# A fused block-sorted attention and PReLU feed-forward kernel: batch 0 without key padding, zeros moved from q to K, and a new instruction order

## The chip, the cores and the metric

The kernel runs on one core of a Trainium2 chip. The metric is device time in microseconds of one execution; lower is better. The engines are PE (matmul), PEld (its weight loads), DVE (vector), ACT (activations), POOL (general) and SP (which only issues DMAs here). "L853" is line 853 of the kernel's source.

## The reference

Attention has 4 batches, 8 heads, 768 positions and 64 dimensions per head. Each head's 8 x 8 matrix is normalised five times (Sinkhorn) and mixes the 8 blocks of 96 keys and values; query block i then attends to mixed block i alone.

```python
for _ in range(5):
    P = P - np.max(P, axis=-1, keepdims=True)
    P = np.exp(P)
    P = P / (np.sum(P, axis=-1, keepdims=True) + 1e-09)
    P = P / (np.sum(P, axis=-2, keepdims=True) + 1e-09)
...
k_sorted = np.einsum('bhij,bhjcd->bhicd', P, k_b).reshape(B, H, S, D)
v_sorted = np.einsum('bhij,bhjcd->bhicd', P, v_b).reshape(B, H, S, D)
...
scores = scale * np.matmul(q_b, k_sb.transpose(0, 1, 2, 4, 3))
scores = scores - np.max(scores, axis=-1, keepdims=True)
attn = np.exp(scores)
attn = attn / (np.sum(attn, axis=-1, keepdims=True) + 1e-09)
return np.matmul(attn, v_sb).reshape(B, H, S, D).astype(np.float32)
...
h = x @ w_in                       # x: 3072 x 512, w_in: 512 x 2048
g = np.maximum(h, 0.0) + alpha * np.minimum(h, 0.0)
return (g @ w_out).astype(np.float32)
```

## The kernel before

**An order written out.** The body does not emit instructions at once. It adds operations to a graph, each with what it reads and writes, and numbers them in the order in which they were added. Three tables then decide everything: `ORDER` lists for each of the five engines the numbers of its operations in the order in which they run, `BANKS` gives each accumulator tile its PSUM bank, and entries such as `11.1` in PE's list are fillers (`filler`, L1009: eleven products of the identity with 512 columns, into bank 1), which only keep PE running. An operation waits for the semaphores of what it depends on, and what stands behind it on its engine waits with it. An operation marked `EITHER` may stand in ACT's list or in DVE's.

**Groups.** There are 32 groups `g` of 96 positions, 8 to a batch. Batch 0 (`near`) and batches 1 to 3 (`far`) take different ways, to start early in the one and to save PE in the other.

**Opening, batch 0.** A first run of `BURST` products of 32 x 32 zeros (L907) and fillers keep PE running. SP loads `sort_net` (`P32`, L402) and `moe_alpha` (`alphaR`, L404). POOL's queue loads q, v and k of batch 0, then k of batch 1, the four row blocks of `w_in`, then v and `w_out`. `consts` (L478 on) builds the identity (DVE memset, POOL select, ACT copy to `identb`) and masks from it by DVE reductions. `sinkhorn` (L552 on) runs five rounds on DVE with one exp on ACT in each, and leaves `Pb`. `spread0` (L584) spreads it with three selectors held in `w_out_bf` until the weights arrive; DVE makes the block matrices `BDQ` (L589) and `BDV` (L594). `prep_q` (L645) transposes q on PE, `prep_k0` (L661) mixes and transposes k in 6 units, and `prep_v` (L716) mixes v in 8 units of 8 products each, with a strided slice of `hT` as weights and 64 moving columns; ACT or DVE copies each result out of PSUM (through the helper at L397). Batch 0 has its 96 keys of a block laid out as 4 x 32, of which 24 are filled; the rest are zeros or copies (L495, L497, L670).

**One group of attention** (`attention`). For batch 0, L755 makes scores with q in rows, DVE takes their maximum (L762, `nm`), L770 makes the scores again transposed, L781 subtracts the maxima by a product with the identity, ACT takes the exp (L801, `ET`), and L812 multiplies by v, with a 65th column for the sum. DVE divides (L817, L820, `xq`) and PE turns the result (L834) into `xT`. For batches 1 to 3, L752 makes scores with full rows: q is staged in `QN` with zeros beside each head (L508), turned by DMA into `QTz` (L440), and multiplied by K of two heads at once, in 8 products of 96 columns. ACT takes the exp (L789), a DMA turns it (L794), and L812 follows. K and v of these batches are prepared by POOL copies into zero-padded stages (`conv_k` L677, `conv_v`), one product per unit (`prep_k` L689, `prep_v` L716) and a copy out of PSUM.

**The feed-forward part** runs in chunks of 192 or 384 positions: `ffn1` (L853 on PE, relu on ACT at L860 into one of three `t1`, then L863 on DVE into `hT`) and `ffn2` (L885, a copy out, and the store at L896). Its steps are set between those of the attention.

Of the kernel before, what the change touches and what calls it, by code (L numbers as in the profile page):

```python
# [13 lines left out]
NB = 8  # L14
# [9 lines left out]
BK = (128, 112)  # L24
LK = 4 * NB * 128
NE = 3
VSL = 4
EPS = 1e-9
BURST = 140
# [13 lines left out]
        723 759 662 894 659 893 890 660 661 889 663 819 787 788 818 918 917""",  # L43
    "sync": """
# [3 lines left out]
        1127 1098 1118 1090 1058 1148 1172 1214 1226 1193 1220 1232""",  # L48
    "pe": """
# [17 lines left out]
        1224 1217 1218 1229 1230""",  # L67
    "act": """
# [10 lines left out]
        1180 1183 1195 1198 1147 1204 1207 1225 1219""",  # L79
    "dve": """  # L80
# [13 lines left out]
        1163 1151 1178 1160 1187 1192 1166 1175 1171 1184 1202 1181 1196 1199 1208 1205 1213 1231""",  # L94
}
BANKS = (
    "0720176402566007103123674545623016702014516040740232332571154023556674710151666723230371765023127466"
    "7345562601566762045563520172323073704233472267005451247552145562703761201777760440167073416745102212"
    "4567503020451227731314512700026654567764370120171140356567274267567010450223343406134451717670102147"
    "562372753011225033452370700112467116304617335716342532617524"  # L100
# [221 lines left out]
def bass_sinkhorn_attn__then__act_prelu_kernel(  # L322
# [40 lines left out]
    one0 = sb("one0", [128, 1], F32)  # L363
# [6 lines left out]
    QN = sb("QN", [128, 6, 8, 128], BF16)  # L370
# [3 lines left out]
    QTz = [sb("QTz%d" % n, [128, 2, 4, S], BF16) for n in range(2)]  # L374
# [38 lines left out]
    d_qn = [dma_sem("qn%d" % h) for h in range(H)]  # L413
# [10 lines left out]
    def load_q(b, prio):  # L424
        if b == 0:
            o, i = quarters(hT, 8192, HR, q)
            G.add(POOL, lambda e: e.dma_start(o, i), load_us, w=[("QS", 0)], prio=prio, dma=(d_q, 0), kind="load")
            return
        for h in range(H):
            G.add(POOL, lambda e, h=h: e.dma_start(  # L430
                AP(QN, h * 128 + (h // 4) * 64, [[6144, 128], [1024, 6], [1, 64]]),
                AP(q.tensor, b * HB + h * S * D, [[D, 128], [128 * D, 6], [1, D]])),
                660, r=[("QN0", h)] + paced(13, h // 2) * (b == 3), w=[("QN", h)], prio=prio,
                dma=(d_qn[h], 0), kind="load")
# [45 lines left out]
    def consts():  # L480
# [26 lines left out]
        for h in range(H):  # L507
            G.add(POOL, lambda e, h=h: e.memset(  # L508
                AP(QN, h * 128 + (1 - h // 4) * 64, [[6144, 128], [1024, 6], [1, 64]]), 0.0),
                430, w=[("QN0", h)], prio=-21)  # L510
# [538 lines left out]
```

## Time and profile before

| | |
|---|---|
| median of 3 runs | 239.11 us (237.74, 239.11, 239.56) |
| the profiled execution's own time | 237.91 us |
| its span, first to last instruction | 236.2 us |
| PE busy | 228.7 us (97%) |
| DVE, ACT, POOL busy | 167.2, 151.8, 104.3 us |
| mean granted PE clock | 0.986 |
| DMA | 31.35 MB, mean 133 GB/s |

The profile is of one execution; 1.7 us of its time lie outside its span. Rows of the timeline and of the chain begin with the start and the length in us, then the engine (in the timeline) or the engine and what is written (in the chain); "x8" is the number of instructions that were merged. A busy PE is not PE at its peak, since ends of products are modelled. In the windows, the clock is the share of the full PE clock that was granted.

### The profile page before, as it was taken

The page shows a single profiled execution, that of the slowest core. Times are in us where ns is not written, and L with a number is a line of the kernel's source. Part 1 is how long each engine was busy: PE and PEld are TensorE (multiplying, and loading weights), DVE is VectorE, ACT ScalarE, POOL GpSimd, SP SyncE. Part 2 cuts the span into 40 slices and gives each one's busy share as a digit, 9 for nine tenths or more (in the row PEclk, how much of TensorE's full clock was granted, in tenths as well). Part 3 has the DMA queues.
Part 4 walks back from the last instruction along what each step waited for, and adds up shares of the span by engine and source line. Part 5 has one row for each costly group of instructions (what it writes and reads, how often), then busy time and mean ns, then how long its engine had stood idle before and what let it go on. Part 6 is the DMA issues. An engine that isn't in the chain of part 4 may idle for free.

```text
span 236.2 us, 5977 instructions
## 1 busy us (share of the span) xinstructions
PE 228.7 (97%) x2379; PEld 144.9 (61%) x2379; DVE 167.2 (71%) x344; ACT 151.8 (64%) x421; POOL 104.3 (44%) x153
## 2 busy tenths in 40 slices
PE   5999989999999999999999999999999999999995
PEld 3469868866566666566665666565655556455553
DVE  5774499997699788896797687684877558634741
ACT  4356648988598796687867758457758564433331
POOL 7939929997399997431778880000000000000000
PEclk9998599999999999999999999999999999999999
DMA  5999999996999999999828999842282691400024
GB/s 82 213 218 208 208 190 209 220 153 46 179 181 132 106 127 181 220 231 180 160 80 84 102 132 143 164 81 51 60 118 75 154 166 44 140 4 0 0 92 179
DMA packets 72381, 31.35 MB, mean 133 GB/s; under 512 B 64528, under 2 KB 67360, under 8 KB 72352
## 3 DMA queue, kind: packets, MB, share of 16 engines
q0 software_dynamic: 23808, 13.63, 42.6%
q1 hardware_dynamic: 48544, 17.33, 36.8%
q8 instruction: 19, 0.31, 0.6%
q14 instruction: 10, 0.08, 0.1%
HBM read 27.28 MB, written 6.29 MB: 142 GB/s over the span
## 4 chain that ended last, share of the span: by engine, by line
PE 82%; DMA 7%; DVE 5%; ACT 3%; issue 1%; SPq 0%; POOLq 0%
PE ps L853 32%; PE ps L885 31%; PE ps L716 4%; PE ps L752 4%; PE ps L812 3%; DMA ET<-Esb 3%; DMA hT<-in_q_dram 3%; PE ps L781 2%; DVE hT L863 2%; PE ps L689 1%; ACT ET L801 1%; DVE outstg L397 1%; PE ps L834 1%; PE ps L755 1%; DMA out_dram<-outstg 1%
## 5 line engine op out<-in xcount | busy, mean ns | idle before, releaser
L863 DVE SCALAR_TENSOR_TENSOR hT<-t,omaT,ps 128x384 bf16<-128x384 f32 (+1 forms) x144 | 76.7, 562 | 30.8 <-ACT t L860 29.1
L853 PE MATMUL ps<-xT,w_in_bf 128*128 128x384 bf16 (+1 forms) x576 | 95.6, 308 | 0.2 <-DVE rec L817 0.2
L885 PE MATMUL ps<-w_out_bf,hT 128*128 128x512 bf16 (+1 forms) x400 | 93.4, 371 | 0.1
L860 ACT ACTIVATE t<-ps 128x384 f32<-128x384 f32 (+1 forms) x144 | 61.5, 458 | 43.8 <-PE ps L853 33.7
L853 PEld LDWEIGHTS ps<-xT,w_in_bf 128*128 128x128 bf16 x576 | 51.8, 98 | 29.6 <-ACT xT L397 0.4
L885 PEld LDWEIGHTS ps<-w_out_bf,hT 128*128 128x128 bf16 x400 | 36.5, 98 | 32.9 <-DVE VS L397 0.2
L789 ACT ACTIVATE Esb<-ps,nf 96x96 bf16<-96x96 f32 x192 | 46.1, 345 | 6.4 <-DVE nf L762 6.2
L397 POOL COPY VDz<-VST 64x384 bf16<-64x384 bf16 x40 | 34.1, 852 | 9.8 <-DMA VST<-in_v_dram 6.0
L677 POOL COPY KSz<-KS 64x512 bf16<-64x512 bf16 x36 | 22.0, 612 | 8.9 <-DMA KS<-in_k_dram 3.6
L762 DVE TENSOR_REDUCE nf<-ps 96x8 f32<-96x768 f32 x24 | 22.7, 948 | 3.5 <-PE ps L752 3.4
L430 POOL DMA_DIRECT2D QN<-in_q_dram x24 | 20.0, 838 | 6.5 <-DMA QTz<-QN 6.5
L820 DVE TENSOR_TENSOR xq<-ps,rec 96x512 bf16<-96x512 f32 x32 | 21.7, 681 | 0.4
L812 PEld LDWEIGHTS ps<-VS,ET 112*128 112x128 bf16 (+1 forms) x256 | 11.4, 99 | 5.2 <-ACT ET L801 0.9
L812 PE MATMUL ps<-VS,ET 112*128 112x65 bf16 (+1 forms) x256 | 13.4, 196 | 1.1 <-ACT ET L801 0.6
L397 DVE COPY outstg<-ps 128x512 f32<-128x512 f32 (+1 forms) x14 | 9.3, 667 | 7.1 <-PE ps L885 4.8
L752 PEld LDWEIGHTS ps<-KT,QTz 128*96 128x96 bf16 x192 | 11.9, 125 | 3.6 <-ACT VS L397 0.5
L397 ACT ACTIVATE VS<-ps 112x512 bf16<-112x512 f32 (+1 forms) x18 | 12.0, 697 | 3.1 <-PE ps L716 2.9
L397 ACT ACTIVATE KT<-ps 128x512 bf16<-128x512 f32 x17 | 9.8, 600 | 4.1 <-PE ps L661 2.4
L752 PE MATMUL ps<-KT,QTz 128*96 128x96 bf16 x192 | 12.4, 208 | 0.0
L817 DVE RECIPROCAL rec<-ps 96x8 f32<-96x8 f32 x32 | 6.3, 200 | 8.3 <-PE ps L812 8.1
L762 DVE TENSOR_REDUCE nm<-ps 96x8 bf16<-96x768 f32 x8 | 7.6, 949 | 5.9 <-PE ps L755 5.8
L397 ACT ACTIVATE outstg<-ps 128x512 f32<-128x512 f32 (+1 forms) x11 | 6.4, 579 | 7.9 <-PE ps L885 7.9
(101 smaller groups left out, 183.6 us busy)
## 6 DMA issues: line engine op xcount, KB each, us to landing
out_dram<-outstg SPq DMA_DIRECT2D x23, 256.0 KB, 2.6
KS<-in_k_dram POOLq DMA_DIRECT2D x3, 768.0 KB, 9.8
QN<-in_q_dram POOLq DMA_DIRECT2D x24, 96.0 KB, 3.7
w_in_bf<-in_moe_w_in_dram POOLq DMA_DIRECT2D x4, 512.0 KB, 9.2
w_out_bf<-in_moe_w_out_dram POOLq DMA_DIRECT2D x2, 1024.0 KB, 16.3
VST<-in_v_dram POOLq DMA_DIRECT2D x4, 384.0 KB, 13.5
hT<-in_q_dram POOLq DMA_DIRECT2D x1, 768.0 KB, 7.3
hT<-in_v_dram POOLq DMA_DIRECT2D x2, 384.0 KB, 6.2
```

The source lines that it names most:

```text
L397: return e.activation(o, i, ACTF.Copy) if e is nc.scalar else e.tensor_copy(o, i)
L430: G.add(POOL, lambda e, h=h: e.dma_start(AP(QN, h * 128 + (h // 4) * 64, [[6144, 128], [1024, 6], [1, 64]]), AP(q.tensor, b * HB + h * S * ...
L677: G.add(POOL, lambda e, hp=hp: e.tensor_copy(AP(KSz, hp * 64 * 3072 + u % 3 * 1024 + hp * 64, [[3072, 64], [128, 8], [1, 64]]), AP(KS[n], ...
L752: inst = e.matmul(o, AP(QTz[n], hp * 3072 + h4 * 768 + i * 96, [[6144, 128], [1, 96]]), AP(KT[n], (h4 * 8 + i) * bk, [[LK, 128], [64, 2], ...
L762: G.add(DVE, lambda e: e.tensor_reduce(AP(nx, 0, [[8, 96], [4, 2], [1, 4]]), AP(ps, X.at(), [[LP, 96], [X.step, 2], [96, 4], [1, 96]]), Ax ...
L789: inst = e.activation(AP(Esb[me], p * 128, [[1024, 96], [64, 2], [1, 48]]), AP(ps, X.at((p % 4) * 96) + p // 4 * X.step, [[LP, 96], [48, 2 ...
L812: inst = e.matmul(AP(ps, Z.at(h4 * 68) + hp * Z.step, [[LP, 128], [1, 65]]), AP(ET[et], pos(h4, hp) * 96, [[800, nk], [1, 128]]), AP(VS[n] ...
L820: G.add(DVE, lambda e: e.tensor_tensor(out=AP(xq[me], 0, [[512, 96], [256, 2], [64, 4], [1, 64]]), in0=AP(ps, Z.at(), [[LP, 96], [Z.step, ...
L853: inst = e.matmul(AP(ps, T.at(), [[LP, 128], [1, n]]), AP(w_in_bf, kt * DFF + ft * 128, [[KT_TILES * DFF, 128], [1, 128]]), AP(xT, kt * XR ...
L860: G.add(ACT, lambda e: e.activation(AP(t1[tb], 0, [[384, 128], [1, n]]), AP(ps, T.at(), [[LP, 128], [1, n]]), ACTF.Relu, scale=-1.0), t_ac ...
L863: G.add(DVE, lambda e: e.scalar_tensor_tensor(out=AP(hT, ft * RING + tok % RING, [[FT_TILES * RING, 128], [1, n]]), in0=AP(t1[tb], 0, [[38 ...
L885: inst = e.matmul(AP(ps, T.at(), [[LP, 128], [1, n]]), AP(hT, ft * RING + tok % RING, [[FT_TILES * RING, 128], [1, 128]]), AP(w_out_bf, ft ...
```

## The change

Seven things change together, and the three tables are written anew (the numbers of operations shift with the body):

- Batch 0 is dense: 96 keys per block with no padding. K of batch 0 is written at stride 24, the POOL copy at L670, the memsets at L497 and the masked column of ones (`one0`, an ACT step) go, and the second scores, the subtraction and the exp take 96 keys where they took 128.
- `prep_v` of batch 0 reads 128 strided columns as weights over 96 keys (the last 32 come from q's part of `hT` and are not used), and seven of the eight products of a unit have 128 moving columns, of which the second 64 are written over by the next product.
- In batches 1 to 3 K and not q is zero-padded: `QN` and the turned q have half their size, `QN` has two buffers, K of two heads stands in 192 columns with zeros (`zero_k`, two POOL memsets per buffer), and the first scores are 4 products of 192 columns where they were 8 of 96. Each copy of a K unit out of PSUM becomes two, of 64 partitions each.
- `spread0` has one PSUM tile and one operation for each of its three selectors.
- `NE` is 4 where it was 3 (buffers of exp, its turned form and `xq`), and `BURST` is 165 where it was 140.
- In the new order SP issues `alphaR` ahead of `sort_net`; DVE has the maximum of `sort_net` ahead of the memset of the identity; 16 of the 48 transposes of q stand ahead of the spread and 32 behind it; the last selector is copied on ACT behind the first copy of q; one of the six units of k stands behind four units of v.
- Fillers are 9, 13 and 2 where they were 11, 11, 3, 1 and 3. POOL has all six `BDM` and `BDV` products of batches 1 to 3, of which DVE had three. Of the K copies of batches 1 to 3 ACT has 25 and DVE 11 (14 and 4 before).

```diff
-BK = (128, 112)
-LK = 4 * NB * 128
-NE = 3
+BK = (96, 192)
+LK = 4 * NB * 192
+NE = 4
-BURST = 140
+BURST = 165
...
-                AP(QN, h * 128 + (h // 4) * 64, [[6144, 128], [1024, 6], [1, 64]]),
+                AP(QN[b % 2], h % 4 * 128 + h // 4 * 64, [[3072, 128], [512, 6], [1, 64]]),
...
-            AP(QTz[n], t * 128, [[6144, 128], [768, 8], [1, 128]]),
-            AP(QN, t * 1024, [[6144, 128], [1, 1024]])),
+            AP(QT[n], t * 128, [[3072, 128], [768, 4], [1, 128]]),
+            AP(QN[n], t * 512, [[3072, 128], [1, 512]])),
...
     def spread0(prio):
-        T = G.bank(1, "P")
-        def f(e):
-            inst = None
-            for x in range(3):
+        T = [G.bank(1, "P") for _ in range(3)]
+        for x in range(3):
+            def f(e, x=x):
+                inst = None
...
-        if u == 1:
-            G.add(POOL, lambda e: e.tensor_copy(AP(KT[0], 24, [[LK, 128], [32, 128], [1, 8]]),
-                                                AP(KT[0], 0, [[LK, 128], [32, 128], [1, 8]])), 1150,
-                  r=[("KT", 0, 0), ("KT", 0, 1)], w=["KTpad"], prio=prio + 0.1)
+    def zero_k(n, prio):
+        z = KT[n].bitcast(F32)
+        for hp in range(2):
+            G.add(POOL, lambda e, hp=hp: e.memset(
+                AP(z, hp * 64 * (LK // 2) + (1 - hp) * 48, [[LK // 2, 64], [96, 32], [1, 48]]), 0.0),
+                1600, w=[("KTz", n, hp)], prio=prio)
...
-        o = AP(KT[n], 8 * u, [[LK, 128], [BK[1], 32], [64, 2], [1, 8]])
-        G.add(EITHER, lambda e: copy(e, o, AP(ps, T.at(), [[LP, 128], [2, 32], [1, 2], [64, 8]])),
-              t_either(512), r=[T], w=[("KT", n, u)], prio=prio)
+        for hp in range(2):
+            G.add(EITHER, lambda e, hp=hp: copy(
+                e, AP(KT[n], hp * (64 * LK + 96) + 8 * u, [[LK, 64], [192, 32], [48, 2], [1, 8]]),
+                AP(ps, hp * 64 * LP + T.at(), [[LP, 64], [2, 32], [1, 2], [64, 8]])),
+                t_either(512), r=[T], w=[("KT", n, u, hp)], prio=prio)
...
+                w = 2 if dd < 7 else 1
+                inst = e.matmul(AP(ps, T.at(dd * 64), [[LP, 128], [1, 64 * w]]),
+                                AP(hT, 8 * u + dd, [[HR, 128], [64, 128]]),
+                                AP(BDV, 0, [[256, 128], [0, w], [1, 64]]))
...
+                if far:
+                    inst = e.matmul(sc(2 * h4, 96, 192), AP(QT[n], h4 * 768 + i * 96, [[3072, 128], [1, 96]]),
+                                    AP(KT[n], (h4 * 8 + i) * bk, [[LK, 128], [1, bk]]))
+                    continue
```

More of the change, by code (lines that the diff above doesn't have):

```diff
@@ L369, in bass_sinkhorn_attn__then__act_prelu_kernel @@
     hT = sb("hT", [128, FT_TILES, RING], BF16)
-    QN = sb("QN", [128, 6, 8, 128], BF16)
+    QN = [sb("QN%d" % n, [128, 6, 4, 128], BF16) for n in range(2)]
     KS = [sb("KS%d" % n, [128, 3072], BF16) for n in range(2)]
@@ L373, in bass_sinkhorn_attn__then__act_prelu_kernel @@
     VDz = sb("VDz", [128, VSL * 8 * 128], BF16)
-    QTz = [sb("QTz%d" % n, [128, 2, 4, S], BF16) for n in range(2)]
+    QT = [sb("QT%d" % n, [128, 4, S], BF16) for n in range(2)]
     KT = [sb("KT%d" % n, [128, LK], BF16) for n in range(2)]
@@ L411, in bass_sinkhorn_attn__then__act_prelu_kernel @@
     load_us = 3720
-    d_qn = [dma_sem("qn%d" % h) for h in range(H)]
+    d_qn = [dma_sem("qn%d" % h) for h in range(2 * H)]
     d_qt = [dma_sem("qt%d" % t) for t in range(6)]
@@ L494, in consts @@
         for th in range(2):
-            G.add(POOL, lambda e, th=th: e.memset(AP(zh, th * 64 * HR // 2 + (1 - th) * 2048, [[HR // 2, 64], [1, 2048]]), 0.0),
-                  1990, w=[("VDo", th)], prio=-95.2)
-            G.add(POOL, lambda e, th=th: e.memset(AP(zh, th * 64 * HR // 2 + th * 2048 + 768, [[HR // 2, 64], [1024, 2], [1, 256]]),
-                                                  0.0), 560, w=[("VDp", th)], prio=-95.2)
+            G.add(POOL, lambda e, th=th: e.memset(AP(zh, th * 64 * HR // 2 + (1 - th) * 1536, [[HR // 2, 64], [1, 1536]]), 0.0),
+                  1450, w=[("VDo", th)], prio=-95.2)
         zv, zk = VDz.bitcast(F32), KSz.bitcast(F32)
@@ L506, in consts @@
             G.add(DVE, lambda e, n=n: e.memset(AP(ET[n], 768, [[800, 128], [1, 32]]), 0.0), 100, w=[("ETp", n)], prio=-88)
[L507 to L510, printed above, removed]
-        G.add(DVE, lambda e: e.memset(AP(VS[1], 64, [[64 * 65, 128], [65, 64]]), 0.125), 110, w=[("VS1", 1)], prio=-30)
+        zero_k(1, -21)
+        for n in range(2):
+            G.add(DVE, lambda e, n=n: e.memset(AP(VS[n], 64, [[64 * 65, 128], [65, 64]]), 0.125), 110, w=[("VS1", n)],
+                  prio=(-69, -30)[n])
         def red(o, src, w, prio=-70, ax=AxisListType.X):
@@ L532, in consts @@
               prio=-67)
-        red(one0[:, :], AP(identf, 0, [[128, 128], [32, 4], [1, 24]]), "one0", -69, AxisListType.XY)
-        G.add(ACT, lambda e: e.activation(AP(VS[0], 64, [[64 * 65, 128], [65, 64]]), AP(one0, 0, [[1, 128], [0, 64]]),
-                                          ACTF.Copy, scale=0.125),
-              490, r=["one0"], w=[("VS1", 0)], prio=-60)
         G.add(ACT, lambda e: copy(e, AP(selk, 0, [[512, 32], [16, 32], [1, 16]]),
@@ L577, in spread0 @@
     def spread0(prio):
-        T = G.bank(1, "P")
-        def f(e):
-            inst = None
-            for x in range(3):
+        T = [G.bank(1, "P") for _ in range(3)]
+        for x in range(3):
+            def f(e, x=x):
+                inst = None
                 for j in range(8):
-                    inst = e.matmul(AP(ps, T.at(x * 8), [[LP, 128], [1, 8]]), AP(w_out_bf, x * 1024 + j * 128, [[WR, 32], [1, 128]]),
+                    inst = e.matmul(AP(ps, T[x].at(), [[LP, 128], [1, 8]]),
+                                    AP(w_out_bf, x * 1024 + j * 128, [[WR, 32], [1, 128]]),
                                     AP(Pb, j, [[64, 32], [8, 8]]), start=(j == 0), stop=(j == 7))
-            return inst
-        G.add(PE, f, 24 * 26, r=["Pb"] + [("sel0", x) for x in range(3)], w=[T], prio=prio, mode=1)
+                return inst
+            G.add(PE, f, 8 * 26, r=["Pb", ("sel0", x)], w=[T[x]], prio=prio, mode=1)
         for x in range(2):
@@ L649, in prep_q @@
         G.add(PE, f, 8 * 58, r=[("QS", 0), "identb"], w=[T], prio=prio, mode=4)
-        G.add(EITHER, lambda e: copy(e, AP(QTz[0], 8 * u, [[6144, 128], [24, 128], [1, 8]]),
+        G.add(EITHER, lambda e: copy(e, AP(QT[0], 8 * u, [[3072, 128], [24, 128], [1, 8]]),
                                      AP(psb, 2 * T.at(), [[2 * LP, 128], [1, 128], [128, 8]])),
@@ L665, in prep_k0 @@
         G.add(PE, f, 4 * 58, r=[("KS", 0), ("KS", 0, 0), ("BDQ", 0), ("BDQ", 1)], w=[T], prio=prio, mode=4)
-        G.add(EITHER, lambda e: copy(e, AP(KT[0], 4 * u, [[LK, 128], [32, 128], [1, 4]]),
+        G.add(EITHER, lambda e: copy(e, AP(KT[0], 4 * u, [[LK, 128], [24, 128], [1, 4]]),
                                      AP(ps, T.at(), [[LP, 128], [1, 128], [128, 4]])),
-              t_either(512), r=[T], w=[("KT", 0, u)], prio=prio)
-        if u == 1:
-            G.add(POOL, lambda e: e.tensor_copy(AP(KT[0], 24, [[LK, 128], [32, 128], [1, 8]]),
-                                                AP(KT[0], 0, [[LK, 128], [32, 128], [1, 8]])), 1150,
-                  r=[("KT", 0, 0), ("KT", 0, 1)], w=["KTpad"], prio=prio + 0.1)
+              t_either(512), r=[T], w=[("KT", 0, u, hp) for hp in range(2)], prio=prio)
+    def zero_k(n, prio):
[4 more added lines that the diff above has]
+                1600, w=[("KTz", n, hp)], prio=prio)
     def conv_k(b, u, prio):
@@ L713, in f @@
             for dd in range(8):
-                z = AP(VDz, (u % VSL * 8 + dd) * 128, [[VSL * 1024, 128], [1, 128]]) if b else \
-                    AP(hT, 8 * u + dd, [[HR, 128], [64, 128]])
-                inst = e.matmul(AP(ps, T.at(dd * 64), [[LP, 128], [1, 64]]), z,
-                                AP(BDV, b * 64, [[256, 128], [1, 64]]))
-            return inst
-        G.add(PE, f, 235 if b else 8 * 60,
-              r=[(x, th) for x in ("VD", "VDo", "VDp") for th in range(2)] * (b == 0) +
-              [("VDz", u % VSL, th) for th in range(2)] * (b > 0) + [("BDV", b)], w=[T], prio=prio)
+                if b:
+                    inst = e.matmul(AP(ps, T.at(dd * 64), [[LP, 128], [1, 64]]),
+                                    AP(VDz, (u % VSL * 8 + dd) * 128, [[VSL * 1024, 128], [1, 128]]),
+                                    AP(BDV, b * 64, [[256, 128], [1, 64]]))
+                    continue
[3 more added lines that the diff above has]
+                                AP(BDV, 0, [[256, 128], [0, w], [1, 64]]))
+            return inst
+        G.add(PE, f, 235 if b else 8 * 89,
+              r=[(x, th) for x in ("VD", "VDo") for th in range(2)] * (b == 0) + [("QS", 0)] * (b == 0) +
+              [("VDz", u % VSL, th) for th in range(2)] * (b > 0) + [("BDV", b)], w=[T], prio=prio, mode=0 if b else 7)
         G.add(EITHER, lambda e: copy(e, AP(VS[n], 8 * u, [[64 * 65, nk], [65, 64], [1, 8]]),
@@ L734, in attention @@
         bk = BK[far]
-        nk = 112 if far else 128
+        nk = 112 if far else 96
         pos = (lambda h4, hp: 2 * h4 + hp) if far else (lambda h4, hp: 4 * hp + h4)
-        kt_keys = [("KT", n, u) for u in range(6)]
-        qt_keys = [("QTzt", n, t) for t in range(i * 96 // 128, (i * 96 + 95) // 128 + 1)] if far else \
+        kt_keys = [("KT", n, u, hp) for u in range(6) for hp in range(2)] + [("KTz", n, hp) for hp in range(2)]
+        qt_keys = [("QTt", n, t) for t in range(i * 96 // 128, (i * 96 + 95) // 128 + 1)] if far else \
             [("Q0", u) for u in range(3)]
@@ L748, in s1 @@
             for h4 in range(4):
+                if far:
+                    inst = e.matmul(sc(2 * h4, 96, 192), AP(QT[n], h4 * 768 + i * 96, [[3072, 128], [1, 96]]),
+                                    AP(KT[n], (h4 * 8 + i) * bk, [[LK, 128], [1, bk]]))
+                    continue
                 for hp in range(2):
-                    o = sc(pos(h4, hp), 96)
-                    if far:
-                        inst = e.matmul(o, AP(QTz[n], hp * 3072 + h4 * 768 + i * 96, [[6144, 128], [1, 96]]),
-                                        AP(KT[n], (h4 * 8 + i) * bk, [[LK, 128], [64, 2], [1, 48]]))
-                    else:
-                        inst = e.matmul(o, AP(QTz[n], hp * 64 * 6144 + h4 * 768 + i * 96, [[6144, 64], [1, 96]]),
-                                        AP(KT[n], hp * 64 * LK + (h4 * 8 + i) * bk, [[LK, 64], [32, 4], [1, 24]]))
+                    inst = e.matmul(sc(pos(h4, hp), 96),
+                                    AP(QT[n], hp * 64 * 3072 + h4 * 768 + i * 96, [[3072, 64], [1, 96]]),
+                                    AP(KT[n], hp * 64 * LK + (h4 * 8 + i) * bk, [[LK, 64], [1, 96]]))
             return inst
-        op = G.add(PE, s1, 360 if far else 180, r=kt_keys + qt_keys, w=[X], prio=ps_, mode=0 if far else 2)
+        op = G.add(PE, s1, 332 if far else 180, r=kt_keys + qt_keys, w=[X], prio=ps_, mode=0 if far else 2)
         if not far:
@@ L797, in attention @@
         else:
-            op = G.add(PE, s2, 190, r=kt_keys + qt_keys + ["KTpad", ("nm", m)], w=[X], prio=ps_, mode=2)
+            op = G.add(PE, s2, 190, r=kt_keys + qt_keys + [("nm", m)], w=[X], prio=ps_, mode=2)
             near.append(op.idx)
@@ L977, in bass_sinkhorn_attn__then__act_prelu_kernel @@
         if g == 7:
-            G.add(DVE, lambda e: e.memset(AP(VS[0], 64, [[64 * 65, 128], [65, 64]]), 0.125), 110,
-                  w=[("VS1", 0)], prio=8)
+            zero_k(0, 9)
         if b + 1 < B:
```

47 lines of the change are left out of this document (23 added, 24 removed), and 97 rows, old and new, of the table ORDER.

## The prediction

> **What bounds the kernel now.** I read the page first, then the windows by stage, then the chain that ended last.
>
> ```profile
> span 236.2 us, 5977 instructions
> PE 228.7 (97%) x2379; PEld 144.9 (61%) x2379; DVE 167.2 (71%) x344; ACT 151.8 (64%) x421; POOL 104.3 (44%) x153
> PE 82%; DMA 7%; DVE 5%; ACT 3%; issue 1%; SPq 0%; POOLq 0%
> ```
> ```profile
> 15.00:20.00 5.00, 4.86 (x82) 4.39 (x76) 3.15 (x7) 3.71 (x6) 2.31 (x4) 1.00 1.03 209
> 20.00:25.00 5.00, 5.00 (x70) 4.64 (x71) 1.34 (x3) 3.23 (x6) 4.75 (x9) 0.67 1.05 206
> 25.00:30.00 5.00, 4.89 (x83) 3.78 (x79) 3.12 (x6) 2.74 (x5) 4.84 (x9) 0.65 1.07 212
> 40.00:50.00 10.00, 9.72 (x146) 7.98 (x145) 9.28 (x24) 8.59 (x21) 9.31 (x15) 1.00 1.26 206
> 50.00:60.00 10.00, 9.83 (x128) 6.51 (x128) 8.44 (x18) 7.46 (x14) 7.44 (x11) 1.00 1.10 74
> 60.00:80.00 20.00, 19.98 (x199) 12.60 (x198) 16.89 (x32) 15.44 (x47) 16.36 (x21) 1.00 1.17 162
> 100.00:120.00 20.00, 20.00 (x191) 12.47 (x190) 16.00 (x32) 15.99 (x51) 8.15 (x12) 1.00 0.96 170
> ```
> The columns are the stretch, its length, busy time of PE, PEld, DVE, ACT and POOL with counts, the granted clock, DMA share and GB/s. Three stages follow. To about 34 us is the opening of batch 0, a chain of small steps; in 20 to 30 us the clock falls to 0.67 and 0.65. From 34 to 60 us the first feed-forward chunks run with DVE at 9.28 and ACT at 8.59 of 10. From 60 us PE is busy 19.98 and 20.00 of 20, so only PE work, or a new wait, moves the end there.
>
> **The opening, up to the sort matrix.** The change issues alphaR ahead of sort_net on SP, and on DVE puts the row maximum of sort_net, which waits for that load, ahead of the memset of identf.
>
> ```profile
> 0.82 0.41 SPq L402 DMA_DIRECT2D P<-in_sort_net_dram  x1
> P<-in_sort_net_dram SPq DMA_DIRECT2D x1, 8.0 KB, 1.7
> 2.21 0.30 POOL L482 TENSOR_SCALAR_AFFINE_SELECT identf<-identf 128x128 f32<-128x128 f32 x1
> 3.29 0.30 DVE L514 TENSOR_REDUCE mkh<-identf 128x16 f32<-128x128 f32 x1
> 3.54 0.24 ACT L563 ACTIVATE P<-P 32x64 f32<-32x64 f32 x1
> 7.68 0.21 DVE L565 TENSOR_REDUCE rs<-P 32x8 f32<-32x64 f32 x1 [0.32 <-ACT P L563]
> 9.44 0.21 DVE L565 TENSOR_REDUCE rs<-P 32x8 f32<-32x64 f32 x1 [0.32 <-ACT P L563]
> 11.45 0.21 DVE L565 TENSOR_REDUCE rs<-P 32x8 f32<-32x64 f32 x1 [0.56 <-ACT P L563]
> 12.69 0.21 DVE L574 TENSOR_TENSOR Pb<-P,cs 32x64 bf16<-32x64 f32 x1
> ```
> P now leaves 0.41 later and lands near 2.98 (0.82 + 0.41 + about 1.7). Behind its maximum stand the memset of identf, then POOL's select (0.30), then the mkh reduction (0.30), which is ahead of the subtraction on DVE; the first exp moves from 3.54 to about 4.4. All of ACT and PE that needs identb waits with it. A clean round takes 1.76 (7.68 to 9.44); the old fourth took 2.01 because ACT was in the first QTz copy. The new order puts that copy behind the fifth exp and two reductions into the fourth round instead, so I take 0.1 back of the 0.9: Pb ends near 13.7 for 12.90, **+0.8**.
>
> **From Pb to v.**
>
> ```profile
> 8.69 1.53 PE L645 MATMUL ps<-identb,hT 128*64 128x128 bf16 x48 [0.30 <-DMA hT<-in_q_dram]
> 10.15 2.55 PE L1009 MATMUL ps<-identb 128*128 128x512 bf16 x11
> 10.26 1.02 ACT L397 ACTIVATE QTz<-ps 128x1024 bf16<-128x1024 bf16 x1 [0.75 <-PE ps L645]
> 14.59 1.64 PE L661 MATMUL ps<-BDQ,KS 128*64 128x128 bf16 x40
> 16.67 2.33 PE L716 MATMUL ps<-BDV,hT 128*128 128x64 bf16 x24
> ```
> Before, all 48 transposes of q ran at 8.69, while Pb was awaited. Now 32 of them stand behind Pb, and the third selector that the spread needs is copied on ACT behind a 1.02 us copy of q. ACT's list after the fifth exp (at about 12.2) is four small steps, that copy and the selector, so the last spread group starts near 14.5, and 16 transposes (0.51) follow it: k starts near 15.3 for 14.59. Between the halves of k stand 16 more transposes, but 8 of its 48 products go behind v and a wait of the old order is filled; v starts near 17.2 for 16.67, **+0.5**. The 8 products that moved come back inside the v stage, **+0.3**.
>
> **v with 128 moving columns, and the clock.**
>
> ```profile
> 23.03 1.56 PE L716 MATMUL ps<-BDV,hT 128*128 128x64 bf16 x16
> 22.40 0.82 PE L781 MATMUL ps<-identb,nm 96*128 96x96 bf16 x8
> 29.07 0.52 PE L781 MATMUL ps<-identb,nm 96*128 96x96 bf16 x8
> 24.87 0.52 PE L770 MATMUL ps<-QTz,KT 64*128 64x96 bf16 x8
> 28.80 0.34 PE L770 MATMUL ps<-QTz,KT 64*128 64x96 bf16 x8
> 24.51 0.55 PE L755 MATMUL ps<-KT,QTz 64*96 64x96 bf16 x8
> 29.52 0.38 PE L755 MATMUL ps<-KT,QTz 64*96 64x96 bf16 x8
> 27.30 0.62 PE L812 MATMUL ps<-VS,ET 128*128 128x65 bf16 x8
> 30.49 0.41 PE L812 MATMUL ps<-VS,ET 128*128 128x65 bf16 x8 [0.59 <-ACT ET L801]
> 33.46 0.65 PE ps L1009 x3
> 34.72 1.32 PE ps L853 x16
> 185.06 0.72 PE ps L752 x16
> ```
> The last three rows are of the chain, the others of the timeline. One product of v takes 97 ns at full clock (2.33 / 24) and 97 at the low one (1.56 / 16). So its 64 columns do not set it, not even when they stream half as fast; the strided weights do. 128 columns at full clock stream as long as 64 at half, so the wider products should fit: **+0.2**, between 0 and 1.7 (64 products by 27 ns, the 64 further columns at L853's 82.5 ns for 192). The array then streams for 55 of 97 ns instead of 27, and I expect no fall of the clock at 21 us. Three passes of L781 (0.30 each), three of L770 (0.16 to 0.18), two of L755 (0.17) and two of L812 (0.21 and 0.09) ran low: **-2.1** for all. But the group's own chain (DVE maximum, ACT exp) does not get faster with PE, and DVE is free for most of 20 to 25 us, so waits appear where PE was slow. Bounds are 0 and the whole 2.1; I give back **+0.9**, a little under half, because PE still has other groups' products between.
>
> The Trainium skill, page "TensorE: Matmul & The Clock Gate", section "What's actually happening", has the clock at one half after an idle window of about 3.4 us; this trace agrees in size (0.67 and 0.65 over 5 us stretches that are partly low), though PE was not idle but thinly filled.
>
> Fillers ahead of the first feed-forward product fall from four to two; at 0.216 each (0.65 / 3) that is **-0.4**. The opening sums to +0.5 + 0.3 + 0.2 - 2.1 + 0.9 - 0.4 = **-0.6**.
>
> **Scores of batches 1 to 3.** Eight products of 96 columns take 0.36 (L752, 45 ns each); four of 192 at L853's 82.5 ns take 0.33. 24 groups: **-0.7**, all on PE's path after 60 us.
>
> That page's section "Weight-path perf modes" gives fast weight loading to 128 columns alone; here batch 0's second scores and subtractions go from 128 to 96. At its 96 / 1.2 = 80 ns each load (an estimate of that page) against 44 in the rows, 128 products would cost up to 4.6 us more. The trace disagrees: L752 loads 96 columns and keeps 45 ns each, so I add nothing.
>
> **K in two halves.** The evacuation of each K unit of batches 1 to 3 becomes two copies of 64 partitions by the same 512 elements.
>
> ```profile
> L397 ACT ACTIVATE KT<-ps 128x512 bf16<-128x512 f32 x17 | 9.8, 600 | 4.1 <-PE ps L661 2.4
> ```
> A copy's time goes with its elements per partition, so I take 600 ns for a half: 18 more, 10.8 us of ACT and DVE. Six fall in 34 to 60 us, 3.6 us, and the new order puts nearly all on ACT; three small BDM/BDV products go from DVE to POOL. Free in 40 to 60 us are 0.72 + 1.56 on DVE and 1.41 + 2.54 on ACT. Bounds: 0 (they fit) and 3.6 (each delays a t1, then hT, then PE); I take **+0.7**. The twelve others meet 3.1 to 4.6 us free per 20 on each engine; **+0.2** for waits on PSUM banks (0 to 1.2).
>
> **At nothing:** the zeroing of q's staging (eight memsets) against four memsets of K on POOL, off the path; the q transposes by DMA halve, and a fourth attention buffer frees SP's queue, but PE did not wait there (20.00 of 20). Without that cover a late q turn would hold the first scores of a batch. The 25 extra opening products only lengthen a wait.
>
> **Sum:** -0.6 - 0.7 + 0.7 + 0.2 = -0.4 on the profiled execution's 237.91 gives 237.5. That execution lies 1.2 below the median of 239.11 and 0.67 below the mean of the four times shown (238.58); I add 0.6 and predict **238.1**, its own range 236.9 to 239.6.
>
> **The rivals.** *The low clock only comes earlier* (240.3). For it: fillers. PE now has 13 fillers from about 9.2, at 0.23 each (2.55 / 11) done by 12.2, and Pb comes at 13.7; until 15.3 only small spreads and transposes run. That is a thin stretch of 3 us just ahead of k. Against: the old clock held at 1.00 in 15 to 20 us, with v thin from 16.67 on. Price: -2.1 is not gained, the +0.9 falls away, transposes and k at half rate cost about 1.0: 238.1 + 2.1 - 0.9 + 1.0. The page on the clock gate, in "Part 4: PE-mode transpose", says that transposes do not count as busy; that speaks for this rival, and no row here shows it.
>
> *K's halves set the pace* (242.0, slower). Place: ACT at 34 to 60 us, in order, between the relu that frees a t1 and the K copies that wait for PE. It decides once ACT's free 3.95 us of 40 to 60 are used up by 3.6 of copies and their waits: then hT is late, and the second product of the feed-forward behind it. Price: the upper bounds 3.6 + 1.2 in place of 0.9. For it: DVE at 9.28 of 10 already. Against: other feed-forward work can stand between.
>
> *All covers hold* (236.3, faster): the clock's gain is whole (-0.9) and K's copies are hidden (-0.9). For it: DVE has 1.34 of 5 busy at 20 to 25 us. Against: every opening chain here waited somewhere.
>
> *The change does not do what it says*, v stays thin for the clock because weight loads, not columns, fill its time: the first rival's place, without the 1.0: 239.3; I count it there.
>
> **How the numbers follow.** Forecast 0.36, low clock earlier or kept 0.15, K's halves 0.23, all covers 0.26. A measurement of this kernel can tell about 1% from no change, so faster is below 236.7, slower above 241.5. Faster: all covers 0.25 and the forecast's edge 0.02, 0.27. Slower: K's halves 0.20 and the low clock's far end 0.05, 0.25. The rest, 0.48, is within 1%. The range goes from 234.8 (all covers, with v's start not late either and a lucky run) to 242.0.
>
> **What would show it.** Right: Pb at 13.5 to 14, v from about 17, granted clock 1.00 through 15 to 30, the first L856 product near 33, L753 at 0.33 per group, PE 20 of 20 from 60 us. Wrong: a clock near 0.5 anywhere after 12 us; Pb by 13; PE under 9.5 of 10 in 40 to 60 with ACT over 9; PE idle after 60 us.

## The result, and the profile after

The changed kernel takes 235.86 us in the median (235.33 to 237.02, four executions) against 239.03 us for the kernel before beside it: a ratio of 0.989, with a 95% interval of 0.9853 to 0.9928. Its profiled execution took 236.1 us, 1.8 less than the profiled one of before; the span fell by 2.0 (236.2 to 234.2). That lies in the predicted range (234.8 to 242.0), 2.2 us below the forecast, and next to the rival "all covers hold" (236.3). It is below the 236.7 at which the prediction drew the line for "faster", and so on a side to which it gave 0.27.

First the page: its span, the busy times, and the shares of the chain that ended last.

```profile
span 234.2 us, 5831 instructions
PE 225.9 (96%) x2303; PEld 143.0 (61%) x2303; DVE 170.6 (73%) x349; ACT 155.2 (66%) x430; POOL 105.8 (45%) x150
PE 87%; DVE 5%; ACT 3%; DMA 2%; POOL 1%; issue 1%; SPq 1%; POOLq 0%
```

PE still sets the end. It is busy for 2.8 us less; DVE and ACT have gained 3.4 each, the second K copies among it, and still end little. The DMA share of the chain fell from 7% to 2%. The same windows as before (columns as there):

```profile
15.00:20.00 5.00, 5.00 (x95) 4.69 (x89) 2.66 (x5) 3.63 (x7) 1.71 (x3) 1.00 1.08 220
20.00:25.00 5.00, 5.00 (x80) 4.63 (x78) 3.91 (x6) 3.14 (x6) 1.98 (x2) 1.00 1.03 209
25.00:30.00 5.00, 4.78 (x105) 3.96 (x105) 4.49 (x8) 3.21 (x4) 4.44 (x6) 1.00 1.05 212
40.00:50.00 10.00, 9.97 (x140) 7.58 (x138) 8.41 (x20) 9.68 (x23) 9.47 (x16) 1.00 1.62 154
50.00:60.00 10.00, 10.00 (x128) 7.01 (x127) 7.55 (x18) 8.65 (x20) 9.34 (x14) 1.00 1.23 134
60.00:80.00 20.00, 19.80 (x190) 12.46 (x189) 16.39 (x30) 16.18 (x52) 16.77 (x24) 1.00 0.94 139
100.00:120.00 20.00, 19.33 (x169) 11.53 (x167) 15.64 (x31) 14.45 (x49) 13.54 (x19) 1.00 1.15 156
```

The clock column is the news: 1.00 where 20 to 30 us had 0.67 and 0.65, and 105 matmuls in 25 to 30 where 83 fitted. In 40 to 60 us PE is fuller than before (19.97 for 19.55) although ACT is at 9.68 of 10 with the K copies. In 100 to 120, PE now idles for 0.67. Rows of the timeline and, behind the dots, one of the chain; then PE's waits from 60 us on:

```profile
4.32 0.26 ACT L556 ACTIVATE P<-P 32x64 f32<-32x64 f32 x1
12.44 1.29 ACT L397 ACTIVATE QT<-ps 128x1024 bf16<-128x1024 bf16 x1
13.16 0.21 DVE L567 TENSOR_TENSOR Pb<-P,cs 32x64 bf16<-32x64 f32 x1
13.43 0.93 PE L576 MATMUL ps<-Pb,w_out_bf 32*128 32x8 bf16 x24 [1.38 <-DVE Pb L567]
13.64 0.29 ACT L397 ACTIVATE w_out_bf<-identf 32x128 bf16<-32x128 f32 x1
14.77 0.62 PE L654 MATMUL ps<-BDQ,KS 128*64 128x128 bf16 x16
16.71 3.05 PE L718 MATMUL ps<-BDV,hT 128*128 128x128 bf16 x32
31.34 0.49 PE L856 MATMUL ps<-xT,w_in_bf 128*128 128x192 bf16 x4
...
60.64 0.33 PE ps L753 x4
```
```profile
PE ps L856 <- DVE outstg L397: 0.6, 1, 0.6
PE ps L685 <- ACT t L863: 0.2, 1, 0.2
```

The first exp starts at 4.32 (4.4 was expected), `Pb` ends at 13.37, k starts at 14.77, v at 16.71 (16.67 before), and a product of v with 128 moving columns takes 3.05 / 32 = 95 ns. The first feed-forward product is 2.70 earlier (34.04 to 31.34). From there to the end of the span the changed kernel needs 202.86 us where the kernel before needs 202.16. So 0.70 of the 2.70 is gone again by the end, although the new scores save as much. Part of the 2.70 is only a new place for work that stood ahead of that product: of the products with v (L812 before, L815 now), 40 stood ahead of it and 24 do now, and the 16 that moved behind it take 0.8 (0.41 for eight). Besides, a copy of an output tile on DVE, itself behind the store that empties its buffer, holds PE for 0.6. The rest is not split.

### The profile page after: what moved, and what is told of

Same layout as the page of the kernel before. It is cut to its first block, busy times and chain, and to the rows that moved or that the text cites. A ratio compares the mean times of both kernels' runs of the same rounds, so it can differ in the third digit from the quotient of the medians.

```text
span 234.2 us, 5831 instructions
## 1 busy us (share of the span) xinstructions
PE 225.9 (96%) x2303; PEld 143.0 (61%) x2303; DVE 170.6 (73%) x349; ACT 155.2 (66%) x430; POOL 105.8 (45%) x150
## 4 chain that ended last, share of the span: by engine, by line
PE 87%; DVE 5%; ACT 3%; DMA 2%; POOL 1%; issue 1%; SPq 1%; POOLq 0%
PE ps L856 35%; PE ps L888 33%; PE ps L815 3%; PE ps L753 3%; PE ps L718 3%; PE ps L713 2%; PE ps L685 2%; DMA out_dram<-outstg 2%; PE ps L784 1%; PE ps L773 1%; ACT Esb L792 1%; PE ps L837 1%; PE ps L757 1%; PE ps L654 1%; DVE xq L823 1%
## 5 line engine op out<-in xcount | busy, mean ns | idle before, releaser
L856 PE MATMUL ps<-xT,w_in_bf 128*128 128x384 bf16 (+1 forms) x576 | 96.6, 308 | 0.7 <-DVE outstg L397 0.6
L888 PEld LDWEIGHTS ps<-w_out_bf,hT 128*128 128x128 bf16 x400 | 37.1, 98 | 32.6 <-ACT KT L397 0.3
L397 ACT ACTIVATE KT<-ps 64x512 bf16<-64x512 f32 (+1 forms) x27 | 15.9, 589 | 3.4 <-PE ps L654 1.7
L815 PEld LDWEIGHTS ps<-VS,ET 112*128 112x128 bf16 (+1 forms) x256 | 11.3, 98 | 4.7 <-ACT ET L804 0.6
L815 PE MATMUL ps<-VS,ET 112*128 112x65 bf16 (+1 forms) x256 | 13.1, 194 | 0.2
L753 PE MATMUL ps<-KT,QT 128*96 128x192 bf16 x96 | 11.9, 246 | 0.0
L397 DVE CAST KT<-ps 64x512 bf16<-64x512 f32 (+1 forms) x15 | 10.2, 684 | 2.2 <-PE ps L654 2.0
L753 PEld LDWEIGHTS ps<-KT,QT 128*96 128x96 bf16 x96 | 9.5, 123 | 3.5 <-DVE hT L866 0.5
L397 DVE CAST VS<-ps 112x512 bf16<-112x512 f32 (+1 forms) x14 | 9.6, 687 | 1.3 <-PE ps L718 0.8
## 6 DMA issues: line engine op xcount, KB each, us to landing
KS<-in_k_dram POOLq DMA_DIRECT2D x3, 768.0 KB, 11.7
```

The costliest lines, as they stand in the source:

```text
L397: return e.activation(o, i, ACTF.Copy) if e is nc.scalar else e.tensor_copy(o, i)
L753: inst = e.matmul(sc(2 * h4, 96, 192), AP(QT[n], h4 * 768 + i * 96, [[3072, 128], [1, 96]]), AP(KT[n], (h4 * 8 + i) * bk, [[LK, 128], [1, ...
L815: inst = e.matmul(AP(ps, Z.at(h4 * 68) + hp * Z.step, [[LP, 128], [1, 65]]), AP(ET[et], pos(h4, hp) * 96, [[800, nk], [1, 128]]), AP(VS[n] ...
L856: inst = e.matmul(AP(ps, T.at(), [[LP, 128], [1, n]]), AP(w_in_bf, kt * DFF + ft * 128, [[KT_TILES * DFF, 128], [1, 128]]), AP(xT, kt * XR ...
L888: inst = e.matmul(AP(ps, T.at(), [[LP, 128], [1, n]]), AP(hT, ft * RING + tok % RING, [[FT_TILES * RING, 128], [1, 128]]), AP(w_out_bf, ft ...
```

## The experiments

**Two single edits: v narrow again, and v wide alone.** Theory: the clock falls in v's stage because narrow products under strided weight loads fill the array too thinly; the width alone holds it. Rival: the width does nothing, the rest of the change does.

```diff
 e1: the changed kernel, every product of v with 64 columns
-                w = 2 if dd < 7 else 1
+                w = 1
 e2: the kernel before, with only this edit
-                inst = e.matmul(AP(ps, T.at(dd * 64), [[LP, 128], [1, 64]]), z,
-                                AP(BDV, b * 64, [[256, 128], [1, 64]]))
+                w = 2 if b == 0 and dd < 7 else 1
+                inst = e.matmul(AP(ps, T.at(dd * 64), [[LP, 128], [1, 64 * w]]), z,
+                                AP(BDV, b * 64, [[256, 128], [0, w], [1, 64]]))
```

> The changed kernel with 64 moving columns in batch 0's v products (as before the change), all else as changed. Theory 'clock': the 128 columns are what keeps the clock at full; with 64 the granted clock falls to about 0.5 to 0.7 somewhere in 15 to 30 us and the time rises by 1.3 to 2.1 us over the changed kernel's 235.9, to 237.2 to 238.0. Rival 'order': the gain is that of the new order and of the dense batch 0; the clock stays at 1.00 and the time at 235.9 within 0.5.

> The kernel before with seven of eight v products of batch 0 widened to 128 moving columns, nothing else. Theory 'clock': the clock stays at 1.00 through 20 to 30 us, v's products still take about 95 ns each, and the time falls by 1.2 to 2.0 us from 239.0. Rival 'order': the clock falls as before, or stays and the waits give it all back; 239.0 within 0.5.

e1: 241.32 us, ratio to before 1.0111 (1.0067 to 1.0155). e2: 237.3 us, ratio 0.9932 (0.9889 to 0.9976). Windows of e1 (the second is cut to the long low stretch), then two windows of the kernel before (its low stretch, and from v's start to the first feed-forward product), and the same two of e2:

```profile
15.00:20.00 5.00, 5.00 (x81) 4.62 (x76) 2.05 (x5) 2.74 (x5) 1.68 (x3) 0.66 1.07 218
22.22:39.27 17.05, 17.05 (x209) 14.62 (x208) 11.16 (x22) 7.00 (x12) 9.23 (x13) 0.50 1.16 206
```
```profile
21.73:28.54 6.81, 6.81 (x96) 5.76 (x96) 2.02 (x3) 3.65 (x7) 6.40 (x11) 0.50 1.06 207
16.67:34.04 17.37, 16.59 (x253) 14.04 (x250) 10.42 (x23) 10.79 (x17) 12.77 (x21) 0.80 1.08 205
```
```profile
21.73:28.54 6.81, 6.22 (x133) 5.33 (x132) 3.92 (x7) 4.95 (x9) 6.40 (x11) 1.00 1.07 214
16.42:31.79 15.37, 14.59 (x254) 12.49 (x250) 10.42 (x23) 10.71 (x17) 12.81 (x21) 1.00 1.05 204
...
31.79 0.50 PE L854 MATMUL ps<-xT,w_in_bf 128*128 128x192 bf16 x4
```

One edit takes the low stretch away: the same 6.81 us hold 133 matmuls for 96, and the first feed-forward product moves from 34.04 to 31.79, nearly as far as under the whole change (31.34). Of these 2.25, 0.25 is there already when v starts (16.42 for 16.67, in e11 below too), where the edit cannot act: `Pb` was spread 0.25 earlier in those executions (12.71 for 12.96). The edit's own part is 2.00, from v's start on (17.37 to 15.37). All of it is busy time of PE (16.59 to 14.59); idle time is 0.78 in both. The 0.6 that PE waits inside e2's 6.81 us, for an exp (`ET`), is no new wait: the kernel before has it at 30.49 (0.59, a row that the prediction shows), behind its low stretch. Taking the edit out of the changed kernel makes it slower than the kernel before: the rest of its order, without the width, has one stretch of 3.4 us at half clock (0.66 in 15 to 20 us) and then one of 17 us. The rival falls in both runs. The price in e1 had been put far too low: 241.32 is 5.5 above the changed kernel, where 1.3 to 2.1 had been expected, since the clock stayed low long after v.

**The old scores in the new order.** e3 is the changed kernel with the first scores of batches 1 to 3 as eight products of 96 columns.

```diff
-                    inst = e.matmul(sc(2 * h4, 96, 192), AP(QT[n], ...
-                                    AP(KT[n], (h4 * 8 + i) * bk, [[LK, 128], [1, bk]]))
+                    for hp in range(2):
+                        inst = e.matmul(sc(2 * h4 + hp, 96), AP(QT[n], ...
+                                        AP(KT[n], (h4 * 8 + i) * bk + hp * 96, [[LK, 128], [1, 96]]))
```

> The changed kernel with the first scores of batches 1 to 3 in 8 products of 96 columns instead of 4 of 192 (same result). If PE sets the pace from 60 us, 24 groups by 0.03 us come back: plus 0.7 us, 236.6. Rival: that part of the gain was already eaten by new waits, 235.9 within 0.3.

237.6 us, ratio 0.9936 (0.9898 to 0.9974). Its profiled span is 1.9 longer than the changed kernel's, at full clock in both; 0.7 of that is the products. PE's waits in it from 34 to 225 us:

```profile
PE ps L857 <- DVE outstg L397: 0.6, 1, 0.6
PE ps L713 <- POOL VDz L397: 0.4, 1, 0.4
PE ps L816 <- DMA ET<-Esb: 0.4, 1, 0.4
PE ps L857 <- DVE hT L867: 0.2, 1, 0.2
PE ps L685 <- ACT t L864: 0.2, 1, 0.2
```

Three of the five are new against the changed kernel (1.0 us). Its runs say how much of that is the edit's: six of the twelve have a mean clock of 0.993 or less, and the six at 0.999 or above have a median of 236.7, where those of the changed kernel have 235.8 (8 runs, in part on another chip). That 0.8 is near the 0.7 that was expected for the products alone, so the 1.0 of waits belongs for the most part to this execution.

**K's halves, in the old order and doubled up in the new one.** e5 is e2 with each K copy of batches 1 to 3 made in two halves by one operation, on the engine that the old order gave it. e6 is the changed kernel with the opening order of e4 (below) and one further small copy (64 x 48 elements, into a spare buffer) ahead of each half.

```diff
 e5
-        G.add(EITHER, lambda e: copy(e, o, AP(ps, T.at(), [[LP, 128], ...
+        def halves(e):
+            inst = None
+            for hp in range(2):
+                inst = copy(e, AP(KT[n], hp * 64 * LK + 8 * u, [[LK, 64], ...
+            return inst
+        G.add(EITHER, halves, ...
 e6
+            def more(e, hp=hp):
+                copy(e, AP(spare, ...48, [[864, 64], [1, 48]]),
+                     AP(ps, hp * 64 * LP + T.at(), [[LP, 64], [1, 48]]))
+                return copy(e, AP(KT[n], ...
```

> The kernel before with the wide v products of batch 0 and, besides, each K copy of batches 1 to 3 made as two copies of 64 partitions on the same engine (18 copies of about 0.6 us more). Compared with the same kernel without the halves (237.3; its feed-forward had 15 us of products behind it at 55.4 us). Theory 'hidden': the same within 0.5, and 15 us of products by 55.9 at the latest. Rival 'K's halves set the pace' (the prediction's): plus 0.9 to 4.8 us, and 15 us of products at 56.3 to 59.

> The reordered opening (sort_net and the identity first, 235.5 us) with 36 further small copies of 48 elements per partition into a spare buffer, one ahead of each half copy of K, at some 0.2 us each, 7 us of ACT and DVE. Theory 'hidden': 235.5 within 0.6, since ACT and DVE have room beside PE. Rival 'K copies are at the limit': plus 1.5 us or more.

e5: 245.51 us, ratio 1.0304 (1.0251 to 1.0357), about 8 us more than e2. e6: 237.54 us, ratio 0.9955 (0.9918 to 0.9993), some 2 us more than e4 on another chip. Windows and waits of PE of e5, then e6's:

```profile
40.00:50.00 10.00, 7.90 (x116) 5.98 (x114) 8.68 (x21) 7.80 (x20) 9.23 (x14) 1.00 1.21 207
...
PE ps L890 <- ACT VS L397: 1.6, 1, 1.6
PE ps L817 <- DMA ET<-Esb: 1.3, 1, 1.3
PE ps L760 <- ACT KT L397: 1.0, 1, 1.0
PE ps L890 <- DVE KT L397: 0.7, 1, 0.7
```
```profile
50.00:60.00 10.00, 9.15 (x123) 6.80 (x124) 8.15 (x18) 8.10 (x22) 9.33 (x14) 1.00 1.33 133
...
PE ps L891 <- DVE hT L869: 0.8, 1, 0.8
```

The rival "K's halves set the pace" names a real mechanism. In the old order PE idles 2.1 of the 10 us from 40 on, 1.1 of it behind K copies and 0.9 behind steps of `hT`, and the clock stays at 1.00; the waits listed are from 34 us to the end. The price is above the upper bound that I gave (3.6 + 1.2): PE waits not only for the K copies but for copies and steps that stand behind them. e5 tests halves that share one place in the list; the changed kernel has a place for each, and 25 of the 36 on ACT. With those, no wait on K is seen; 36 more small copies (0.20 each in the trace) already cost some 2 us, so "hidden" within 0.6 was missed and the limit was nearer. The new order hides the halves with little to spare.

**A version that beats both: sort_net first.** e4 is the changed kernel with `sort_net` loaded ahead of `alphaR`, the row maximum behind the memset of the identity, POOL's select for the identity ahead of the loads of v and k, the third selector ahead of the first q copy on ACT, and 12 fillers for 9.

```diff
 SP    -1 0 171 ...               +0 1 171 ...
 DVE   -2 26 45 14 8 30 46 ...    +2 8 14 26 45 46 30 ...
 POOL  -4 7 5 9 16 ...            +4 9 7 5 16 ...
 ACT   -... 75 43 40 44 29 93 42  +... 75 43 42 44 40 29 93
 PE    -3 9.1 92 13.1 ...         +3 12.1 92 13.1 ...
```

> The changed kernel with sort_net loaded ahead of alphaR, the identity built ahead of the maximum, the third selector copied on ACT ahead of the q copy, and 12 fillers first instead of 9. Theory that Pb sets the opening: Pb about 0.7 us earlier (12.6 to 12.7), the first feed-forward product 0.4 to 0.7 earlier, time 235.2 to 235.5. Rival, that the landing of k and v's strided weights set it: k's mixing starts at 14.4 at the earliest and the time stays at 235.9 within 0.3.

> The changed kernel with sort_net loaded first and 13 fillers, once more, on the chip of the runs beside it. Theory (the earlier sort matrix is worth 0.3 us and a clock that falls less often): 235.0 to 235.8 as on the first chip, ratio to before 0.983 to 0.990. Rival (its 0.6% over the changed kernel was luck of the chip): ratio 0.990 to 0.996, with runs at a clock of 0.985 and 238 us.

e4: 235.49 us (235.01 to 235.8), ratio 0.9863 (0.9828 to 0.9898). The second time, e10: 235.43 us (235.17 to 236.92), ratio 0.9844 (0.9791 to 0.9897). Rows of e4's timeline:

```profile
12.15 1.03 PE L576 MATMUL ps<-Pb,w_out_bf 32*128 32x8 bf16 x24 [0.43 <-DVE Pb L567]
14.38 0.64 PE L654 MATMUL ps<-BDQ,KS 128*64 128x128 bf16 x16 [0.63 <-DMA KS<-in_k_dram]
31.01 0.49 PE L856 MATMUL ps<-xT,w_in_bf 128*128 128x192 bf16 x4
```

`Pb` is spread 1.28 earlier than in the changed kernel (12.15 for 13.43), yet k starts only 0.39 earlier: now it waits for k's own load, as the rival said. That load lands at 14.2 here and at 14.4 in the changed kernel (11.1 us after its issue at 3.10, and 11.7 after 2.69). 0.33 of it is left at the first feed-forward product. That is why the late `Pb` of the changed kernel cost so little. Over runs without a fall of the clock, e4 and e10 have a median of 235.37 (11 runs) and the changed kernel 235.84 (8 runs), 0.5 more; the rest of the lead is that falls are rarer, as the next runs show.

**Does the low clock come back?** e7 is the changed kernel once more on another chip. e8 has 3 fillers for 13 ahead of `Pb`. e9 is e4 with 15 for 13.

> The changed kernel once more, unchanged, beside the others on one chip. Theory 'clock': 235.3 to 237.0, with the runs at the upper end those in which the clock fell for one or two stretches of 3.4 us; so 0.3 to 0.6 above the reordered opening. Rival: the two are the same within 0.2.

> The changed kernel with 3 fillers instead of 13 between the first transposes of q and the spread, so PE is idle from about 9.8 to 13.4 us. Theory of the prediction's first rival (a thin stretch ahead of k makes the clock fall): the clock is low for 3.4 or 6.8 us from about 12 to 16 us on in most runs and the time is 1 to 3 us longer, 237 to 239. If only v's thin stretch matters: no fall after 16 us, 235.9 within 0.5.

> The changed kernel with sort_net loaded first, its row maximum behind the memset of the identity, and 15 fillers where it has 13 (they end 0.43 us before the spread in the run with 13). Theory (the falls of the clock come from the thin stretch between the last filler and k, so that filling 0.43 us more of it makes them rarer): median 235.0 to 235.8, mean clock 1.00 in nearly every run, and no run above 237. Rival (a fall that comes in some runs does not hang on these 0.43 us): the same share of runs above 236.5 as without the two fillers, median equal to that within 0.3.

e7: 237.05 us (235.59 to 238.85), ratio 0.9949 (0.9917 to 0.9981). e8: 237.5 us, ratio 0.9954 (0.9921 to 0.9987). e9: 235.75 us (235.02 to 237.53), ratio 0.9863 (0.9797 to 0.9929). Rows of e7's timeline and windows, then e8's:

```profile
13.44 0.94 PE L576 MATMUL ps<-Pb,w_out_bf 32*128 32x8 bf16 x24 [1.66 <-DVE Pb L567]
14.93:18.33 3.40, 3.40 (x61) 3.02 (x56) 0.69 (x1) 1.31 (x4) 1.77 (x3) 0.50 1.06 214
32.00:35.39 3.39, 3.39 (x30) 2.77 (x31) 2.41 (x7) 1.51 (x3) 1.42 (x3) 0.50 1.15 197
```
```profile
13.43 0.95 PE L576 MATMUL ps<-Pb,w_out_bf 32*128 32x8 bf16 x24 [3.46 <-DVE Pb L567]
11.43:18.24 6.81, 4.81 (x93) 4.52 (x95) 2.94 (x14) 3.48 (x10) 5.16 (x7) 0.50 1.08 217
```

This is the first rival, in its place: behind a thin stretch ahead of k, here 1.66 us of idle PE (1.38 in the profile that did not fall) and then small spreads and transposes, the clock falls for 3.4 us in this execution. It falls a second time from 32.00 on, with PE busy before it for 3.13 of 3.40 us; the first profile of the same kernel has no fall there with 3.22 of 3.40, so the cause of the second fall is open. Whether a run falls differs from run to run of one kernel. A stretch of 3.4 us at half clock takes 0.007 off a run's mean clock (half of 3.4 over 236), so each run can be counted: at 0.999 or above were 8 of 16 runs of the changed kernel, 11 of 12 of e4 and e10, 3 of 12 of e8, none of six of e1, and none of the 60 runs of the kernel before beside these experiments (0.957 to 0.986). These counts do not tell where in a run the clock fell. With the wait for `Pb` lengthened to 3.46 us (e8), the fall is the rule, and in its profile the first feed-forward product comes at 33.15, 1.8 later than in the changed kernel's. e9's two further fillers did not make falls rarer (two of six runs at 0.993, one above 237): that guess is not borne out, and which part of the stretch between 12 and 14.8 us counts stays open.

**The single edit once more.**

> The kernel before with 128 moving columns in seven of eight products of v of batch 0, and nothing else, once more. Theory (holding the clock in 20 to 30 us is nearly all that the whole change brings): 235.5 to 237.3, ratio 0.988 to 0.994, equal within 0.4% to the changed kernel's 0.989 and 0.995. Rival (the rest of the change is worth over 0.5% beside it): over 1.2 us slower than the other kernels of this call.

e11: 237.31 us, ratio 0.9894 (0.9829 to 0.9958): the changed kernel's own 0.989, but 1.9 us above e10 beside it (which also has e4's opening), with the clock at 1.00 in all its six runs. Here the stated rival is nearer. PE's waits from 60 us on and the timeline of its profiled execution (237.9 us) show what the rest of the change is good for:

```profile
PE ps L753 <- DMA QTz<-QN: 1.6, 1, 1.6
PE ps L854 <- DVE rec L818: 0.8, 1, 0.8
...
97.17 7.22 SPq L440 DMA_TRANSPOSE QTz<-QN  x3
106.25 0.53 PE L753 MATMUL ps<-KT,QTz 128*96 128x96 bf16 x8 [1.56 <-DMA QTz<-QN]
```

Three turns of q fill SP's queue for 7.22 us, and the first scores of a batch wait. The profiled execution of the same kernel as e2 had 0.3 there. The changed kernel turns half the bytes from two buffers, and no wait of PE on a turn of q stands in its list. Over the runs at a clock of 0.999 or more, the median is 236.9 for e2 and e11 (14 runs) and 235.8 for the changed kernel (8 runs, in part on another chip): in runs that hold the clock, the rest of the change is worth about 1.0. But the single edit holds it in 14 of 16 runs and the whole change in 8 of 16, and by all runs the two are not told apart: the ratios to the kernel before are 0.9932 and 0.9894 for the edit, 0.989 and 0.9949 for the change.

## Why the prediction was right, and where it was off

The main mechanism, the clock, was right, and the time lies in a wide range; the sum was 2.2 too high, since the costs that were to take gains back (waits, v's late start, K's halves) came out near nothing. By its own terms:

- **Clock, -2.1: right in size, and the largest term.** e2 gives -2.00 from v's start to the first feed-forward product for this edit alone, v's own width included. The Trainium skill, page "TensorE: Matmul & The Clock Gate", section "What's actually happening", knows two clock states, one half and full, switched after windows of about 3.4 us that run freely; the rows agree (0.50 over 3.40, 6.81 and 17.05 us), and free windows would explain why one kernel falls in half of its runs, though no run here sets their phase. It speaks of idle windows. Here PE is busy for 6.81 of 6.81 us from 21.73 to 28.54, and for 3.40 of 3.40 before that.
- **Waits that give back +0.9: the step that failed first.** No new wait came: PE idles for 0.78 between v's start and the first feed-forward product in the kernel before and in e2, and the wait for an exp is the same 0.6 in both. The group's own chain, which was to hold PE up, did not hold it up further.
- **v's width +0.2 (0 to 1.7): the low end.** 95 ns for 128 columns against 97 for 64: the strided weights set both. The same 128 x 64 product with weights side by side (L713, batches 1 to 3) takes 50 (0.40 us for eight).
- **v's start +0.5: measured +0.04.** `Pb` came 0.47 late, not 0.8, and the selector, behind which the last spread group was put near 14.5, ran at 13.64, since the q copy ahead of it had begun at 12.44. Most of the lateness was hidden by k's load, which lands at 14.4 (e4).
- **Fillers -0.4 and moved k products +0.3:** in the first feed-forward product's 2.70 there is room for both; they were not measured alone.
- **Scores -0.7: right in size** (0.33 per group); e3's runs at full clock give 0.8.
- **K's halves +0.7 and +0.2: measured nothing** in 40 to 60 us (PE 9.97 and 10.00 of 10). Later a wait of 0.6 appears, but behind an output store, not behind K. The rival's mechanism holds in the old order, at 8 us.
- **At nothing: q's turns.** Hidden in the profile that I had, but e11 shows 1.6 us of them in another execution. The cover that I named was thinner than 20.00 of 20 told.
- **The standing of the profiled run, +0.6: wrong to carry over.** Part of the spread of the kernel before comes with its clock (237.0 us at 0.985, 242.2 at 0.957). The changed kernel's median is below its own profiled execution, which had no fall.

Of the rivals, "all covers hold" (0.26, the forecast had 0.36) came nearest, and by its own two terms: the clock's gain was whole, and K's copies were hidden. Of the signs named, the clock at 1.00 and 0.33 per group came; the first feed-forward product came at 31.34 and not near 33, and PE did idle after 60 us, which had been named a sign of being wrong. "The low clock only comes earlier" is borne out in part: half of the runs have a fall, and e7's profile, the only one of the changed kernel with falls, has the first at 14.93. The price is lower than 240.3: with one or two stretches the changed kernel takes 236.45 to 238.85. So the faster by 1.1% of the first comparison and the 0.5% of e7 are one kernel.

## What to carry to other kernels

Where the granted clock is under 1 in a stage with PE busy, look at how much of each product's time the array streams: widening the moving operand under a slow weight load cost nothing here and was worth 2.0 us in the profile, while all other edits gave about 1.0 in runs that held the clock, and the new order held it less often. Read the clock of every run, not of one profile, before a few tenths of a per cent are put down to an edit. Copies that fit in one order of an engine's list can cost 8 us in another, so price them by the order that they will stand in.

## What had not been expected of the hardware

- PE without a gap can still lose the clock: with 27 of 97 ns streamed in v's products (64 columns, at L853's 82.5 ns for 192) it fell in 60 of 60 runs, with 55 of 97 it held in 14 of 16 runs of the single edit. e1 and e2 vary the columns alone; that the share of time streamed is what the clock follows is a reading of them.
- A low stretch can be long: e1, with 64-column products and the new order, stayed at 0.50 for 17.05 us on end, far past its last product of v, which starts at 25.3. What kept it low is not shown.
- One kernel's runs differ by 3% (the kernel before: 237.0 to 244.9, at mean clocks of 0.957 to 0.986). The clock does not order them alone: 237.0 has 0.985, and 240.81 has 0.986.
